# An attention kernel's score products as 32-row tiles, with zero products in TensorE's gaps, VectorE's exponentials in threes as E + E·v, and another start

## The chip, the cores and the metric

One Trainium2 chip; the program runs on one of its cores. The metric is the device time of one execution, in microseconds (us). The kernel before was run three times: 943.21, 945.67 and 946.64, median 945.67.

## The reference

Two attention blocks over the same input x (2048 rows of 512) are mixed by a gate: a softmax attention A with 32 heads of 16 and a linear attention B. Cut to what matters:

```python
q, k, v = ...                                   # x @ wqkv, 32 heads of 16
p = softmax(einsum("bhqd,bhkd->bhqk", q, k) * 16**-0.5)   # 32 x 2048 x 2048
a = einsum("bhqk,bhkd->bhqd", p, v) @ wo        # block A
...
phi = lambda t: where(t > 0, t + 1, exp(t)) + 1e-6        # block B, linear
o = (phi(q) @ (phi(k).T @ v)) / (phi(q) @ sum(phi(k)) + 1e-6)
g = sigmoid((x * gate_w).sum(-1))
return g * a + (1 - g) * (o @ wo_b)
```

Nearly all the work is in A: 32 x 2048 x 2048 = 134 million exponentials, and for each head a product with only 16 rows of contraction on the way in and only 17 columns (16 of v and a one, whose sum is the softmax's denominator) on the way out.

## The kernel before, in words

**Units.** The work of A is cut into 2048 units. A unit is one head, one block of 128 keys and one chunk of 512 queries: a score product with 128x512 results in one PSUM bank, the exponential of these 65,536 numbers, and four products with v (one for each 128 queries) that add into one PSUM bank, `acc`. 32 rounds of 64 units (4 heads, 16 key blocks) follow one another: 4 groups of eight heads (`t8`), 4 query chunks (`qc`), 2 halves (`half`). At a round's end VectorE divides by the sums (`round_end`, L942 to L971), and only then may the next round write `acc`.

**Score products.** K of eight heads lies on 128 partitions, 16 for each head (`KT`). Q of the four heads of a round is copied by DMA into `Qpad`, where the rows of other heads are zero, so that a product over 64 partitions (`ROWT = 64`, L20) picks one head out (`head_of` L146, `unit_aps` L893). Units that follow each other lie in different halves of TensorE's rows, and two such products can run side by side.

**Two ways to an exponential.** ScalarE takes units three at a time, a *group*: three score products into three banks (`SLOTS`, two sets of three), one `activation(Exp)` over 128x1536 into `PT` (L1337), then the v products from `PT`. VectorE takes the others, called *claims*: one score product into bank 7 (the one bank that is left, `MISC`), an eviction to fixed point (`YI`, L1084), and for each *pair* of claims four instructions over 128x1024 (`close_pair`, L1090): from the upper half of each number a power of two `E` (L1100), from the lower half a cubic polynomial in two steps `pol` (L1102, L1104), and the last step with the product by `E`, which gives `DP` (L1106). Then v products from `DP`.

**Who sets the order.** All instructions are written out by a planner in Python that keeps a clock for every engine (`PE.t`, `AC.t`, `DV.t`), estimated durations (L156 to L167: `LAT`, `QK3_T`, `PV_T`, `d_psum`, `d_sb`) and the time at which each buffer is written and read. On the chip each engine runs its own list in order; semaphores hold it where data is missing. The main loop (from L1306) takes one group a turn: the score products of group g, its activation, and then, as long as TensorE's planned clock is before the time `t_lim` at which the other three banks come free (L1346), it puts in other TensorE work. v products come first (`pv_step`, L984, 12 products for three units), then `misc_step` (L1208): a piece of a projection or of block B (`step_K`, `step_Q`, `step_V`, `step_BK` and so on, held in chains with a due group each) or a claim. Both need bank 7. A claim is made only while VectorE's planned backlog is under `CLAIM_LOAD` = 4.0, and from a round that has `MIN_LEFT` = 24 units left, from its end backwards. `pump` (L401) chooses VectorE's next instruction.

```python
            t_lim = max(max(r_bank[nb0 + k].tr for k in range(nbn)) + LAT, PE.t + 0.02)
            while PE.t < t_lim - 0.05:
                pump(PE.t)
                if pv_step(PE.t):
                    continue
                if PE.t + 0.2 < t_lim and g > last_stage and misc_step(PE.t):
                    continue
                PE.t += 0.05
```

**Start.** Half of x comes by plain DMAs on ScalarE's queue (`xnat`, which lies in `phiQT`) and is transposed on TensorE, half by eight transposing DMAs on SP's queue; then come the weights (L500 to L515). While the first 14 groups run, the projections of the other three quarters of x are put between them (`stage_fns`, L1269), and the gate's 64 products with one column each after group 13. TensorE's first work is 8 products of a zero tile (`warm`, L1253).

**End.** After the last activation come 28 products of the output projection for the last four blocks of 128 rows, the last transposes, four evictions and four stores (L1366 to L1404).

All TensorE products are issued at L490 (L493 for transposes), so the profile tells them apart by the names of their tiles.

Of the kernel before, what the change touches and what calls it, by code (L numbers as in the profile page):

```python
# [19 lines left out]
ROWT = 64  # L20
PVN = 64


A3, A2, A1, A0 = 0.07802452, 0.22606714, 0.69583353, 0.99992521
# [5 lines left out]
POLY_B = A2 / A3 * 2.0 ** 16  # L30
POLY_C = A1 / A3 * 2.0 ** 32
POLY_D = A0 / A3 * 2.0 ** 48
# [113 lines left out]
def head_of(half, j):  # L146

    if ROWT == 128:
        h = 4 * half + j
        return h, 0, j  # L150
    if ROWT == 64:
        return 2 * j + half, 64 * (j // 2), j % 2
    return 2 * j + half, 32 * j, 0


LAT = 0.13  # L156
MM512 = 0.216
QK3_T = {32: 0.25, 64: 0.43, 128: 0.65}[ROWT]
PV_T = 0.115
# [6 lines left out]
def d_sb(n, rate=1.0):  # L166
    return 0.10 + n * 1.042e-3 * rate  # L167


def bass_gated_mix__mha_block__linear_attn_block__prompt_kernel(  # L170
# [20 lines left out]
    NPT = 5  # L191
    NDP = 4
    NQS = 4
    NOUTT = 4

    with ExitStack() as es:
# [19 lines left out]
        pidx_i = SB([128, 1], I32, "pidxi")  # L216
        hidx_f = SB([128, 1], FP32, "hidxf")
        mtmp = SB([128, 8], FP32, "mtmp")
        maskK = SB([128, 8], FP32, "maskK")
        maskQ = SB([128, 4], FP32, "maskQ")  # L220
# [3 lines left out]
        NQI = ROWT // 32  # L224
        Qpad = SB([128, NQS, NQI, 512], BF16, "Qpad")
        VW = 32 if PVN == 64 else 18
        Vraw = SB([128, 2 * NTB * 8 * VW + 32], BF16, "Vaug")
        Vaug = Vraw[:, 0:2 * NTB * 8 * VW].rearrange("p (a t h c) -> p a t h c", a=2, t=NTB, h=8)
        PT = SB([128, NPT, 1536], BF16, "PT")
        YI = SB([128, 2, 1024], I32, "YI")  # L230
        E16 = SB([128, 2, 1024], I16, "E16")
        pol = SB([128, 2, 1024], FP32, "pol")
        DP = SB([128, NDP, 1024], BF16, "DP")
# [5 lines left out]
        upool = SB([128, 2, 512], BF16, "upool")  # L239
        phiK = SB([128, 2, 4, D], BF16, "phiK")  # L240
# [4 lines left out]
        phiQT = SB([128, 2, NCC, 512], BF16, "phiQT")  # L245
# [22 lines left out]
        semXN = [SEM("s_xn0"), SEM("s_xn1")]  # L268
        semW0 = SEM("s_w0")
# [16 lines left out]
        r_xnat = [R(f"xnat{i}") for i in range(2)]  # L286
        r_wA, r_wA0, r_warm, r_wB, r_woA, r_woB = R("wA"), R("wA0"), R("warm"), R("wB"), R("woA"), R("woB")
        r_gw, r_ident, r_const, r_mask, r_bmask, r_dummy = R("gw"), R("ident"), R("const"), R("mask"), R("bmask"), R("dm")
        r_KT = [[R(f"KT{p}_{t}") for t in range(NQC)] for p in range(2)]
        r_Qs = [R("Qs0"), R("Qs1")]  # L290
        r_Q = [R(f"Q{s}") for s in range(NQS)]
        r_V = [[R(f"V{p}_{v}") for v in range(NQC)] for p in range(2)]
        r_PT = [R(f"PT{i}") for i in range(NPT)]
        r_YI = [R("YI0"), R("YI1")]
        r_E16 = [R("E0"), R("E1")]
        r_pol = [R("pol0"), R("pol1")]
# [6 lines left out]
        r_u = [R("u0"), R("u1")]  # L303
# [3 lines left out]
        r_phiQT = [[R(f"phiQT{p}_{i}") for i in range(NCC)] for p in range(2)]  # L307
# [161 lines left out]
        def pe_macro(fns, reads=(), writes=(), dur=0.2):  # L469
            settle(reads, writes)  # L470
            st = est_start(PE, reads, writes)
# [9 lines left out]
            for res in writes:  # L481
                res.w = ev
                res.r = {}
                res.tw = st + dur + 0.05
                res.we = PE
            PE.t = st + dur
            return ev

# [10 lines left out]
        for hh in range(2):  # L499
            dma(xnat[:, hh * (NTB // 2):(hh + 1) * (NTB // 2), :],  # L500
                x2[hh * (S // 2):(hh + 1) * (S // 2), 128 * (NCC - NCP):D].rearrange("(tb p) c -> p tb c", p=128),
                semXN[hh], writes=[r_xnat[hh]], total_after=16, E=AC, lands=6)
        for k3 in range(3):
            dma(wA0[:, :, k3, :], wsrc[:, :, k3 * D:k3 * D + 128], semW0, writes=[], total_after=48, E=AC)
        r_wA0.w = _Raw(semW0, 48)
        r_wA0.tw = 11.0
        dma(gw[:], gate_w.rearrange("(cc p) -> p cc", p=128), semG, writes=[r_gw], total_after=16, noncontig=True, E=AC,
            lands=12)
        NCD = NCC - NCP
        for t in range(NQC):  # L510
            for cc in range(NCD):
                dma(xT[:, cc, 512 * t:512 * (t + 1)], x2[512 * t:512 * (t + 1), 128 * cc:128 * (cc + 1)], semXT[cc][t],
                    writes=[r_xT[cc][t]], total_after=16, transpose=True, E=SP, lands=5 + 1.2 * (2 * t + cc))
        dma(wA[:], wsrc, semW1, writes=[r_wA], total_after=16, lands=20)
        dma(wB[:], B_wqkv.rearrange("(cc p) n -> p cc n", p=128), semW2, writes=[r_wB], total_after=16, lands=24)  # L515
        dma(woA[:], A_wo.rearrange("(i p) n -> p i n", p=128), semW3, writes=[r_woA], total_after=16, lands=26)
        dma(woB[:], B_wo.rearrange("(i p) n -> p i n", p=128), semW4, writes=[r_woB], total_after=16, lands=28)
        xt_all = [r_xT[c][t] for c in range(NCC) for t in range(NQC)]

        def xt_of(t):  # L520
            return [r_xT[c][t] for c in range(NCC)]

# [6 lines left out]
        op(PO, lambda: nc.gpsimd.iota(pidx_i[:], [[0, 1]], base=0, channel_multiplier=1), writes=[r_const])  # L529
# [102 lines left out]
        def w_of(t8, kind, early):  # L632
            if early:
                return (lambda cc: wA0[:, cc, kind, :]), r_wA0
# [835 lines left out]
```

## Time and profile before

| what | value |
|---|---|
| profiled execution, its own time | 949.2 us |
| its span, first to last instruction | 947.4 us |
| ScalarE busy | 862.7 us, 91% |
| TensorE busy (products) | 858.0 us, 91% |
| VectorE busy | 742.3 us, 78% |
| mean granted TensorE clock | 0.969 |
| first activation of a group starts / last one ends | 16.88 / 935.43 us |
| groups on ScalarE; units claimed by VectorE | 611; 215 |
| ScalarE waits for TensorE, in all | 64.6 us, 107 times |
| VectorE waits for a claim's product, in all | 127.1 us, 118 times |

The table of groups gives for each line of the kernel, engine and pair of tiles the number of instructions, their busy time, the mean of one in ns and the idle time of the engine ahead of them. The page's row of digits shows the span in 40 slices, with a row for the clock that TensorE was granted. The view of stages gives the same for any stretch, with the busy time and, after "x", the instructions of each engine; its last three columns are the granted clock, the share of the DMA engines and GB/s. The view in order of time gives the start, the length, the engine and line, the tiles and the count of like instructions that follow one another. Busy times of products overlap each other: what one costs TensorE is read from one start to the next.

### The profile page before, as it was taken

To read this page: it belongs to the slowest core of one execution; us is meant where nothing else is said; L and a number is where in the kernel's file an instruction comes from. 1 tells how busy PE (TensorE), PEld (TensorE's weight loads), DVE (VectorE), ACT (ScalarE), POOL (GpSimd) and SP (SyncE) were. 2 spreads that over 40 slices of the span, in tenths; PEclk is the share of its full clock that TensorE was granted. 3 is DMA by queue.
4 is the path that set the end of the run, shared out by engine and by line. 5 is a ranking of instruction groups with operands and counts; after the bars stand their busy time and mean duration, and the time that the engine had idled before them with its cause. 6 is when DMAs were issued, how large, how long until landed. Compare 5 with 4: busy or idle time off the path is not lost. (4 is left out here: it accounts for less than half of the span.)

```text
span 947.4 us, 25379 instructions
## 1 busy us (share of the span) xinstructions
PE 858.0 (91%) x11144; PEld 422.3 (45%) x11244; DVE 742.3 (78%) x982; ACT 862.7 (91%) x648; POOL 8.8 (1%) x46
## 2 busy tenths in 40 slices
PE   7998988998999898999999988999998999988997
PEld 2544444444444444454444444444444444344443
DVE  4269787778888878878878988877888988687872
ACT  2789899999999989999999999979999999999995
POOL 3000000000000000000000000000000000000000
PEclk7989899999999999999999999979999999999999
DMA  9000000000000000000000001000010011000001
GB/s 277 10 8 7 7 1 10 5 7 6 3 12 2 9 6 7 7 2 7 4 10 7 2 14 23 13 2 7 7 24 14 18 19 29 18 19 12 12 13 35
DMA packets 33902, 16.52 MB, mean 17 GB/s; under 512 B 25664, under 2 KB 32768, under 8 KB 33792
## 3 DMA queue, kind: packets, MB, share of 16 engines
q1 hardware_dynamic: 29600, 13.45, 5.7%
q8 instruction: 89, 1.46, 0.7%
q10 hardware_dynamic: 4192, 1.44, 0.6%
q14 instruction: 21, 0.17, 0.1%
HBM read 5.64 MB, written 2.10 MB: 8 GB/s over the span
## 5 line engine op out<-in xcount | busy, mean ns | idle before, releaser
L1337 ACT ACTIVATE PT<-ps 128x1536 bf16<-128x1536 f32 x611 | 846.6, 1458 | 67.1 <-PE ps L490 64.6
L490 PE MATMUL ps<-Qpad,KT 64*128 64x512 bf16 x2048 | 418.4, 390 | 14.2 <-DVE YI L1084 8.3
L490 PEld LDWEIGHTS ps<-Vaug,PT 128*128 128x128 bf16 x7332 | 255.7, 99 | 251.9 <-PE ps L490 232.7
L490 PE MATMUL ps<-Vaug,PT 128*128 128x64 bf16 x7332 | 330.3, 196 | 5.1 <-DVE Osb L968 0.5
L1084 DVE TENSOR_SCALAR YI<-ps 128x512 int32<-128x512 f32 x215 | 147.8, 687 | 127.9 <-PE ps L490 127.1
L490 PEld LDWEIGHTS ps<-Qpad,KT 64*128 64x128 bf16 x2048 | 83.9, 94 | 142.3 <-issue 64.2
L1104 DVE SCALAR_TENSOR_TENSOR pol<-pol,YI 128x1024 f32<-128x1024 f32 x108 | 131.4, 1216 | 2.8
L1106 DVE SCALAR_TENSOR_TENSOR DP<-pol,E 128x1024 bf16<-128x1024 f32 x108 | 131.0, 1213 | 1.0
L1102 DVE SCALAR_TENSOR_TENSOR pol<-YI 128x1024 f32<-128x1024 uint16 x108 | 130.9, 1212 | 0.0
L1100 DVE TENSOR_SCALAR E<-YI 128x1024 int16<-128x1024 int16 x108 | 74.6, 690 | 3.4
L490 PE MATMUL ps<-Vaug,DP 128*128 128x64 bf16 x860 | 45.2, 195 | 27.1 <-DVE DP L1106 13.2
L490 PEld LDWEIGHTS ps<-Vaug,DP 128*128 128x128 bf16 x860 | 32.6, 98 | 64.0 <-DVE DP L1106 32.2
L490 PE MATMUL ps<-wB,xT 128*128 128x512 bf16 x96 | 31.2, 379 | 10.0 <-DVE YI L1084 6.4
L490 PE MATMUL ps<-xT,wA 128*128 128x512 bf16 x83 | 27.3, 385 | 8.4 <-DVE YI L1084 4.6
L742 DVE COPY tpool<-ps 128x512 f32<-128x512 f32 x32 | 21.9, 683 | 2.9 <-PE ps L490 2.9
L490 PE MATMUL ps<-wA,xT 128*128 128x128 bf16 x192 | 19.5, 226 | 1.8 <-DVE YI L1084 0.6
L875 DVE CAST outt<-ps 128x512 bf16<-128x512 f32 x12 | 8.3, 691 | 16.2 <-PE ps L490 16.2
L701 DVE CAST Vaug<-ps 128x512 bf16<-128x512 f32 x16 | 11.0, 687 | 12.1 <-PE ps L490 12.1
L739 ACT ACTIVATE epool<-tpool 128x512 bf16<-128x512 f32 x32 | 20.2, 631 | 0.2 <-DVE tpool L742 0.2
L490 PE MATMUL ps<-xT,wB 128*128 128x512 bf16 x49 | 15.8, 379 | 3.8 <-DVE YI L1084 2.5
L490 PE MATMUL ps<-woB,OBT 128*128 128x512 bf16 x51 | 15.6, 379 | 4.1 <-DVE YI L1084 3.0
L644 DVE CAST KT<-ps 128x512 bf16<-128x512 f32 x16 | 11.0, 684 | 8.3 <-PE ps L490 8.3
(72 smaller groups left out, 243.5 us busy)
## 6 DMA issues: line engine op xcount, KB each, us to landing
out_dram<-outt SPq DMA_DIRECT2D x16, 128.0 KB, 1.7
Qpad<-Qs SPq DMA_DIRECT2D x124, 16.0 KB, 1.8
wA<-in_A_wqkv_dram SPq DMA_DIRECT2D x1, 1536.0 KB, 7.1
wB<-in_B_wqkv_dram SPq DMA_DIRECT2D x1, 1536.0 KB, 10.4
phiQT<-in_A_x_dram ACTq DMA_DIRECT2D x2, 512.0 KB, 4.9
woA<-in_A_wo_dram SPq DMA_DIRECT2D x1, 512.0 KB, 11.4
woB<-in_B_wo_dram SPq DMA_DIRECT2D x1, 512.0 KB, 12.5
outt<-in_A_wqkv_dram ACTq DMA_DIRECT2D x3, 128.0 KB, 5.5
```

Source lines behind the costliest of these rows:

```text
L490: return lambda: nc.tensor.matmul(o, lhsT=l, rhs=r, start=start, stop=stop, skip_group_check=sg)
L644: push(1, [(lambda: nc.vector.tensor_copy(KT[:, par, 512 * t:512 * (t + 1)], bank_ap(b)), [r_bank[b]], [r_KT[par][t]], d_psum(512), None)])
L701: push(1, [(lambda: nc.vector.tensor_copy(Vaug[:, par, 4 * v:4 * v + 4, :, 0:16], src), [r_bank[b]], [r_V[par][v]], d_psum(512), lambda: v ...
L739: _emit(AC, lambda: nc.scalar.activation(epool[:, s, :], tpool[:, s, :], ACT.Exp), [r_t[s]], [r_e[s]], 0.6, 0.53)
L742: (lambda: nc.vector.tensor_copy(tpool[:, s, :], bank_ap(b)), [r_bank[b]], [r_t[s], r_e[s]], d_psum(512), after),
L875: push(1, [(lambda: nc.vector.tensor_copy(outt[:, s, :], bank_ap(b)), [r_bank[b]], [r_outt[s], r_wA0], d_psum(512), lambda: store_out(tb))])
L1084: push(1, [(lambda: nc.vector.tensor_scalar(YI[:, yi, 512 * k:512 * (k + 1)], bank_ap(b), Y_LO * FRAC, Y_HI * FRAC, op0=ALU.max, op1=ALU.min),
L1100: (lambda: nc.vector.tensor_scalar(e16, hi, float(EXP_OFF + 127), 128.0, op0=ALU.add, op1=ALU.mult), [r_YI[yi]], [r_E16[yi]], d_sb(n, 0.5) ...
L1102: (lambda: nc.vector.scalar_tensor_tensor(out=pl, in0=lo, scalar=POLY_B, in1=lo, op0=ALU.add, op1=ALU.mult), [r_YI[yi]], [r_pol[yi]], d_sb ...
L1104: (lambda: nc.vector.scalar_tensor_tensor(out=pl, in0=pl, scalar=POLY_C, in1=lo, op0=ALU.add, op1=ALU.mult), [r_YI[yi], r_pol[yi]], [r_pol ...
L1106: (lambda: nc.vector.scalar_tensor_tensor(out=DP[:, dp, 0:n], in0=pl, scalar=POLY_D, in1=e16.bitcast(BF16), op0=ALU.add, op1=ALU.mult), [r ...
L1337: op(AC, lambda slot=slot, b0=b0, n=n: nc.scalar.activation(PT[:, slot, 0:n], ps[:, 512 * b0:512 * b0 + n], ACT.Exp, scale=LN2 / FRAC, bia ...
```

## The change

- **Score products** run over 32 partitions (`Qpad` is 512 columns for a round, one mask) in place of 64. The units of a group are three of the four heads j, so they lie in three of the four row tiles.
- **Claims** are of key blocks 12 to 15 only. A claim may be issued right behind a group's three products, of a head in the fourth row tile (`claim_beside`); one by itself is made only at a lower backlog (`LATE_CLAIM` 2.5). A round must have 38 units left (30 the last), where it was 24.
- **VectorE's arithmetic**: three claims make a *triple*, with instructions over 128x1536. The polynomial is normalised so that the exponential is E·D + E·v with a constant D: `pol` (one `scalar_tensor_tensor`), E, v = (pol + C)·lo (another one), and w = v·E as a `tensor_tensor` on bf16. The sum is made by TensorE: a claim's v products are run twice, with E against `V2` (v times D, a second copy that is written for key blocks 12 to 15) and with w against `Vaug`.
- **Zero products**: where the planner has time before `t_lim` and the planned products of the last 3 us fill less than `MAC_LOW` = 0.45 of it, it adds a product of the zero tile into `acc` (`fill`), 512 columns over 128 rows. It can't while `acc` is between rounds.
- **Order**: new estimates of durations; a latest time `t_late` for other work ahead of a group's products; `misc_step` goes ahead of `pv_step` unless more than 12 units wait for their v products; six `PT` buffers for five, three `DP` of three units for four of two.
- **Start**: the first 512 rows of x come whole in one DMA on ScalarE's queue (into two `PT` buffers) and are transposed on TensorE, with copies by VectorE and ScalarE in turn; first weights in three DMAs ahead of all else on SP's queue; the other rows as before, in smaller pieces; the first K is evicted by ScalarE; GpSimd makes the masks with selects and does most of the memsets; 9, 4 and 2 zero products stand around the first projections.
- `phiQT` now lies in `phiK`; `upool` is gone (in place in `epool`).

```diff
-ROWT = 64
-A3, A2, A1, A0 = 0.07802452, 0.22606714, 0.69583353, 0.99992521
+PB, PC, PD = 2.8964260871, 8.9161113650, 12.8125
+NTRI = 3
+KB2 = 12
-LAT = 0.13
-QK3_T = {32: 0.25, 64: 0.43, 128: 0.65}[ROWT]
-PV_T = 0.115
+LAT = 0.11
+QK_T = 0.324
+PV_T = 0.12
+SWITCH_T = 0.095
...
+        def pe_macro(fns, reads=(), writes=(), dur=0.2, mac=0.0, rows=128):
             settle(reads, writes)
+            if rows < pe_rows[0]:
+                PE.t += SWITCH_T
+            pe_rows[0] = rows
...
         def unit_aps(r, u):
             t8, qc, half = rounds[r]
-            kb, j = unit(r, u)
-            h, row, i = head_of(half, j)
-            kt = KT[row:row + ROWT, t8 % 2, 128 * kb:128 * (kb + 1)]
-            q = Qpad[row:row + ROWT, r % NQS, i, :]
+            kb, j = u // 4, u % 4
+            kt = KT[32 * j:32 * j + 32, t8 % 2, 128 * kb:128 * (kb + 1)]
+            q = Qpad[32 * j:32 * j + 32, r % NQS, :]
...
             push(3, [
-                (lambda: nc.vector.tensor_scalar(e16, hi, float(EXP_OFF + 127), 128.0, op0=ALU.add, op1=ALU.mult),
-                 [r_YI[yi]], [r_E16[yi]], d_sb(n, 0.5), None),
                 (lambda: nc.vector.scalar_tensor_tensor(out=pl, in0=lo, scalar=POLY_B, in1=lo, op0=ALU.add, op1=ALU.mult),
-                 [r_YI[yi]], [r_pol[yi]], d_sb(n), None),
-                (lambda: nc.vector.scalar_tensor_tensor(out=pl, in0=pl, scalar=POLY_C, in1=lo, op0=ALU.add, op1=ALU.mult),
-                 [r_YI[yi], r_pol[yi]], [r_pol[yi]], d_sb(n), None),
-                (lambda: nc.vector.scalar_tensor_tensor(out=DP[:, dp, 0:n], in0=pl, scalar=POLY_D, in1=e16.bitcast(BF16),
-                                                        op0=ALU.add, op1=ALU.mult),
-                 [r_pol[yi], r_E16[yi]], [r_DP[dp]], d_sb(n), None)])
+                 [r_YI[yi]], [r_pol], d_sb(n), None),
+                (lambda: nc.vector.tensor_scalar(e16, hi, float(EXP_OFF + 127), 128.0, op0=ALU.add, op1=ALU.mult),
+                 [r_YI[yi]], [r_E16[dp]], d_sb(n, 0.5), None),
+                (lambda: nc.vector.scalar_tensor_tensor(out=w, in0=pl, scalar=POLY_C, in1=lo, op0=ALU.add, op1=ALU.mult),
+                 [r_YI[yi], r_pol], [r_DP[dp]], d_sb(n), None),
+                (lambda: nc.vector.tensor_tensor(w, w, eb, ALU.mult), [r_DP[dp], r_E16[dp]], [r_DP[dp]], d_sb(n, 0.5), None)])
             for k, (r, u) in enumerate(us):
-                pv_pending.append((r, u, DP[:, dp, 512 * k:512 * (k + 1)], r_DP[dp]))
+                sl = slice(512 * k, 512 * (k + 1))
+                pv_pending.append((r, u, [(eb[:, sl], True), (w[:, sl], False)], r_DP[dp]))
...
+        def fill(now):
+            if acc_n[0] == 0 or r_acc.pend:
+                return False
+            pe_macro([f_mm(acc, warm[:, 0:128], warm[:, 0:512], start=False, stop=False, sg=True)], reads=[r_warm],
+                     writes=[r_acc], dur=MM512, mac=0.216)
+            return True
...
             t_lim = max(max(r_bank[nb0 + k].tr for k in range(nbn)) + LAT, PE.t + 0.02)
+            t_late = max(t_lim, AC.t - (QK_T + SWITCH_T + 0.06 + LAT + MARGIN))
             while PE.t < t_lim - 0.05:
                 pump(PE.t)
-                if pv_step(PE.t):
+                behind = sum(1 for e in pv_pending if len(e[2]) == 1) > PV_LAG
+                if behind and PE.t + 0.3 < t_late and pv_step(PE.t):
                     continue
-                if PE.t + 0.2 < t_lim and g > last_stage and misc_step(PE.t):
+                if g > last_stage and misc_step(PE.t, t_late):
+                    continue
+                if not behind and PE.t + 0.3 < t_late and pv_step(PE.t):
+                    continue
+                if PE.t + 0.25 < t_lim and mac_share(PE.t) < MAC_LOW and fill(PE.t):
                     continue
                 PE.t += 0.05
```

## The prediction

> **What bounds the kernel now.** I read the page's busy shares first, then the groups, then the order of time in a good and in a bad stretch, then stages. Whole-page shares put ScalarE and TensorE level:
>
> ```profile
> span 947.4 us, 25379 instructions
> PE 858.0 (91%) x11144; PEld 422.3 (45%) x11244; DVE 742.3 (78%) x982; ACT 862.7 (91%) x648; POOL 8.8 (1%) x46
> ...
> PEclk7989899999999999999999999979999999999999
> ...
> L1337 ACT ACTIVATE PT<-ps 128x1536 bf16<-128x1536 f32 x611 | 846.6, 1458 | 67.1 <-PE ps L490 64.6
> L490 PE MATMUL ps<-Qpad,KT 64*128 64x512 bf16 x2048 | 418.4, 390 | 14.2 <-DVE YI L1084 8.3
> ...
> L1084 DVE TENSOR_SCALAR YI<-ps 128x512 int32<-128x512 f32 x215 | 147.8, 687 | 127.9 <-PE ps L490 127.1
> ```
>
> ScalarE's activations are the long chain, and what they wait for is TensorE; so do VectorE's claims. How fast ScalarE could go is seen where nothing holds it:
>
> ```profile
> 924.58 10.85 ACT L1337 ACTIVATE PT<-ps 128x1536 bf16<-128x1536 f32 x8
> ...
> 928.93 0.60 PE L490 MATMUL ps<-Qpad,KT 64*128 64x512 bf16 x3
> 929.46 0.41 PEld L490 LDWEIGHTS ps<-Vaug,PT 128*128 128x128 bf16 x12 [0.42 <-PE ps L490]
> 929.46 0.52 PE L490 MATMUL ps<-Vaug,PT 128*128 128x64 bf16 x12
> 929.80 0.13 PEld L490 LDWEIGHTS ps<-woA,OT 128*128 128x128 bf16 x2
> ```
>
> Eight activations in 10.85 us, the last one 1.46 long: (10.85 - 1.46)/7 = 1.34 from start to start, since they overlap by 0.12. The median start-to-start over the trace is 1.33; I use 1.335. The whole span then divides so: 16.9 us to the first activation; 611 x 1.335 = 815.7; 32 activations of block B at 0.63 less the overlap, 16.3; 12.0 after the last one (935.4 to 947.4); the rest, 86, is lost between activations. By the stage they fall in (distance between starts, less 1.335): 14.5 up to 60 us, 18.5 in and around the stretches where the clock is halved, 53 over the other 564 groups, 0.094 a group. The page's 64.6 us of waits is less than this, as each break also loses the overlap.
>
> TensorE from one start to the next, at full clock: three score products 929.46 - 928.93 = 0.53, their v products 0.34 to 0.36, so 0.89 of 1.335 for a group; a claim's product 0.2 and its v products 0.12, 0.35 of them a group (215/611), 0.11; projections and block B about 96 us over 611 groups, 0.16. That makes 1.16, spare 0.17: any piece of 0.53 (two products of 512 columns) in the wrong place makes the next group late. That is the bound: ScalarE, held up by a nearly full TensorE.
>
> The bad stretch, in windows of 3.41 us (the granted clock is the third number from the end; it changes only at multiples of this length):
>
> ```profile
> 619.60:623.01 3.41, 3.09 (x49) 1.66 (x50) 1.66 (x3) 3.41 (x3) 0.00 (x0) 1.00 0.01 2
> 623.01:626.43 3.42, 3.02 (x44) 1.40 (x41) 3.35 (x5) 3.42 (x4) 0.00 (x0) 1.00 0.02 5
> 626.43:629.84 3.41, 2.36 (x28) 1.01 (x27) 3.07 (x6) 3.41 (x3) 0.00 (x0) 1.00 0.00 0
> 629.84:633.26 3.42, 3.30 (x35) 1.82 (x35) 0.00 (x0) 1.38 (x2) 0.00 (x0) 0.50 0.00 0
> ```
>
> At a round's end TensorE idles 1 us for `acc`, and the clock halves for 10.2 us. I counted in each such window the products' columns times their share of the 128 rows (512 columns over 128 rows fill 0.219 us: two take 0.528, one 0.309). The six windows of the main loop ahead of a fall are filled to 0.23 to 0.35; of the windows between, none under 0.376; their median is 0.61. So in this trace the clock falls when less than about 0.36 of the array's time is filled, although TensorE is 70% busy in that window.
>
> **The change, part by part.**
>
> 1. Score products. A pair in different halves costs one stream: four products take 0.54, three 0.53, so 0.219 each stream and 0.1 fixed. Three row tiles side by side should be 0.53 - 0.219 = 0.32. Bounds: 0.32, and 0.53 if they don't overlap further. A claim behind them rides in the fourth tile, 0 to 0.2. v products stay 0.36; a claim's are doubled, 0.24. With 0.43 claims a group: 0.32 + 0.36 + 0.10 + 0.16 = 0.94 of 1.335. Spare 0.39 for 0.17.
>
> 2. Waits of ScalarE. With twice the spare room and a latest time for other work, 0.094 a group should shrink, between 0 and 0.094. The nearest row is today's best stage, 240 to 300 us: 42 groups and 4 activations of block B in 60 us lose 1.9 us, 0.045 a group. I take 0.05: 53 becomes 29. What is late next there is `acc` at the round's end, unchanged.
>
> 3. VectorE. A pair costs 2 x 0.687 + 0.690 + 1.212 + 1.216 + 1.213 = 5.705, 2.85 a unit. Triples, from the rows at 1024 and 512 columns (0.693 and 0.417; 1.217 and 0.69): E 0.96, the two three-operand steps 1.745 each, evictions 2.06. The bf16 product isn't in the trace: 0.96 if it runs like E (two-byte, SBUF), 1.745 if like the three-operand steps; I take 0.96, as its operands are two-byte like E's. Sum 7.47, 2.49 a unit (2.75 the other way). VectorE's other work is 742.3 - 615.7 = 126.6. In 110 to 340 us it is busy 190 of 230, and 37 of the idle 40 is the wait for a claim's product; with claims that cost TensorE no turn I take 0.87 of some 870 us: 757 - 120 = 637, 256 units. At today's 0.826: 240; at 0.93 some 276; at the dear product and 0.826, 217. So (2048 - 256)/3 = 597 groups (591 to 610): 14 x 1.335 = 18.7 less. The second V copy, 4 x 0.69 on VectorE, is in the 120.
>
> 4. Clock. Filled per group after: 3 x 0.055 for scores, 0.33 for v, 0.43 x (0.055 + 0.22) for claims, over 1.40, plus projections 0.11: 0.54 on average for 0.60 before, nearer to 0.36. The zero products cost TensorE 0.22 each in time that is spare by the plan, and lift poor windows; they can't run while `acc` changes hands, which is where it fell. Cost of a cold us today: 2.3 lost for 3.4, 5.7 for 10.2, so 0.6. The loss of 18.5 may go to 0 or stay; I take 10.
>
> The rule against this: TensorE: Matmul & The Clock Gate (The HAM clock gate; HAM oscillation) has the clock fall after an idle window of about 3.4 us. By it neither kernel would fall in the main loop, and the loss would be 0, 10 us better than my sum. The windows above contradict it: the longest gap there is 1 us. And TensorEngine Tiling (Key Properties) says that a change of tiling mode drains TensorE. The fixed 0.1 above agrees; this kernel pays it already, in each group, and full-height zero products beside the 32-row ones would only add turns in spare time.
>
> 5. Start. Today: transposes at 5.05, then 3.7 us until VectorE is through its memsets and the copies, first projection at 9.40, eight cold products of 0.5, first activation 16.88. After: x whole at 5.0 to 5.6 (today's x loads land in 4.9 of issue at 0.73), four sets of transposes and copies to 7.0, Q 0.9 (1.7 cold), K 0.9 (1.7), eviction 0.7, score products to activation 0.65 (1.07), 0.2 between. 10.4 warm, 12.4 cold; I take 11.0, 5.9 less. SP's transposing DMAs now stand behind three weight loads, some 3 us later, and are needed two groups later than the first activation; ScalarE's two copies and one eviction lie ahead of its first group.
>
> 6. First 60 us: 14.5 lost, part of it cold. The same stretch's warm groups lose 0.5 for a K step, 1.2 for a V step, 1.4 for the gate: three of each and the gate, 6.5; I take 7 (5 to 14.5). End: unchanged, 12.0 (up to 17 if VectorE's last triple, 5.4 us, comes late).
>
> **Sum**, for the profiled execution: 11.0 + 597 x 1.335 (797.0) + 16.3 + 7 + 10 + 29 + 12.0 = 882.3 of span. Before, the execution took 949.2 for 947.4 of span, and the median of the runs lies 3.5 under it: 882.3 + 1.8 - 3.5 = 881.
>
> **Rivals.**
>
> - *The waits stay* (0.22): the plan's clocks and the chip's differ as before, or `acc` and bank 7 hold things up rather than TensorE's fill. Then 0.094 a group, 18.5 for the clock and 10 for the start stay, claims gain only VectorE's cheaper arithmetic at the dear end (606 groups) and the first activation is at 12: 12 + 809 + 16.3 + 10 + 18.5 + 53 + 12 - 1.7 = 929. For it: best stretches are already without loss. Against: 36.8 us of 37 are VectorE waiting for TensorE.
> - *The clock stays down* (0.08), the one that ends slower: 32-row products fill so little that the zero products, barred between rounds, don't hold 0.36. At 0.6 a cold us, the 66 gained are gone after 110 us more of it (12% of the span); with a quarter of the span cold, 881 + 0.6 x 200 = 1001. For it: 0.54 for 0.60, and falls at round ends. Against: windows without projections have the most spare time, and one zero product a group lifts a window by 0.16.
> - *The gain is no gain* (0.05): the row tiles don't overlap further (0.53 stays), doubled v products take what claims gave back, and VectorE gets no more units: within 10 us of today.
>
> Chances: forecast 0.65. Faster by over 0.5% (about what a measurement of this kernel can tell from none): 0.65 + 0.22 = 0.87; within 0.5% 0.04; slower 0.08 + 0.01. Range: low end from 10.4 + 591 x 1.335 + 16.3 + 5 + 0 + 17 (0.03 a group) + 12 - 1.7 = 848; high end the first rival, 930.
>
> **What would show it.** Three score products to the next start 0.32, not 0.53. Starts of activations 1.335 apart for most, breaks well under 141. About 256 claims, 85 triples, the bf16 product at 0.96. First activation near 11. A clock at 1.0 from the start on; falls, if any, at round ends. I am wrong if the page's clock row shows many digits under 9, if ScalarE waits for TensorE over 50 us in all, or if VectorE stays near 0.8 busy.

## The result, and the profile after

The changed kernel takes 886.05 us in the median of four runs (884.01 to 888.74). The kernel before, on the same chip, takes 946.15 (943.21 to 954.32). The ratio is 0.9354, with an interval of 0.929 to 0.9417. The forecast was 881, with a range of 848 to 930. Medians and ranges count every run; the ratios leave out those more than 1.5% above the kernel's quickest.

The profiled execution took 884.01 us for a span of 882.3. The page, with the lines that answer to those shown of before:

```profile
span 882.3 us, 27338 instructions
PE 783.2 (89%) x12209; PEld 447.8 (51%) x12311; DVE 729.9 (83%) x909; ACT 839.1 (95%) x642; POOL 9.1 (1%) x19
...
PEclk8889999999999999999989999999999999999999
...
L1402 ACT ACTIVATE PT<-ps 128x1536 bf16<-128x1536 f32 x602 | 823.9, 1490 | 23.1 <-PE ps L504 19.9
L504 PE MATMUL ps<-Qpad,KT 32*128 32x512 bf16 x2048 | 275.8, 389 | 34.5 <-ACT PT L1402 15.5
L1098 DVE TENSOR_SCALAR YI<-ps 128x512 int32<-128x512 f32 x244 | 167.5, 687 | 81.5 <-PE ps L504 80.9
...
L1116 DVE SCALAR_TENSOR_TENSOR pol<-YI 128x1536 f32<-128x1536 uint16 x82 | 143.0, 1744 | 2.6
L1120 DVE SCALAR_TENSOR_TENSOR DP<-pol,YI 128x1536 bf16<-128x1536 f32 x82 | 142.4, 1736 | 0.0
...
L1118 DVE TENSOR_SCALAR E<-YI 128x1536 int16<-128x1536 int16 x82 | 77.3, 943 | 0.0
L1122 DVE TENSOR_TENSOR DP<-DP,E 128x1536 bf16<-128x1536 bf16 x82 | 77.2, 941 | 0.2
```

ScalarE is at 95%, and its wait for TensorE has gone from 64.6 to 19.9 us: it is the bound almost alone now (802 of the 882 us are its whole groups at their own pace, see the table below). VectorE takes 244 units for 215, and its wait for a claim's product went from 127.1 to 80.9 us. Its four steps of a triple cost 943, 941, 1744 and 1736 ns in the mean. The clock row has its digits under 9 at the start and one in the middle.

A good stretch in order of time, 202 to 219 us:

```profile
202.21 0.10 PEld L504 LDWEIGHTS ps<-warm 128*128 128x128 bf16 x1 [0.35 <-PE ps L504]
...
202.53 0.10 PEld L504 LDWEIGHTS ps<-Qpad,KT 32*128 32x128 bf16 x4 [0.23 <-issue]
202.54 0.40 PE L504 MATMUL ps<-Qpad,KT 32*128 32x512 bf16 x4
...
202.87 0.52 PE L504 MATMUL ps<-Vaug,PT 128*128 128x64 bf16 x12
...
207.74 14.98 ACT L1402 ACTIVATE PT<-ps 128x1536 bf16<-128x1536 f32 x11
```

Four score products, three of a group and one of a claim behind them, start at 202.54 and the next product at 202.87: 0.33 us, where three took 0.53. Not all fours are as short: half of them take 0.41 us or more. A zero product stands ahead of them in TensorE's free time. The eleven activations in 14.98 us are (14.98 - 1.46)/10 = 1.35 apart: ScalarE runs through.

Dividing both profiled spans in the same way, each loss being the distance between activations' starts less 1.335:

| term of the span, us | before | forecast | after |
|---|---|---|---|
| to the first activation | 16.9 | 11.0 | 13.2 |
| whole groups x 1.335 | 611: 815.7 | 597: 797.0 | 601: 802.3 |
| block B's activations, one short group | 16.3 | 16.3 | 18.5 |
| lost before 60 us | 14.5 | 7 | 11.7 |
| lost at a halved clock, after 60 us | 18.5 | 10 | 4.0 |
| other losses after 60 us | 53 | 29 | 18.4 |
| after the last whole activation | 12.0 | 12.0 | 14.1 |
| sum | 947 | 882.3 | 882.2 |

Of the 65 us between the spans, 35 are waits, 14.5 the clock, 13.4 ten groups fewer, and the start gives 6.6; block B and the end cost 4.3 more. The sum agrees with the forecast far better than its terms do; the misses are taken up below.

Where a number below is called the fill of a window, it is counted as in the prediction, by weight loads (their records are complete; some products' are missing): columns times rows, 0.219 us for 512 columns over 128 rows, in windows of 3.41 us aligned with the clock's changes.

### The profile page after: what moved, and what is told of

Read it like the earlier page. It is cut to its first block, busy times and chain, and to the rows that moved or that the text cites. A ratio compares the mean times of both kernels' runs of the same rounds, so it can differ in the third digit from the quotient of the medians.

```text
span 882.3 us, 27338 instructions
## 1 busy us (share of the span) xinstructions
PE 783.2 (89%) x12209; PEld 447.8 (51%) x12311; DVE 729.9 (83%) x909; ACT 839.1 (95%) x642; POOL 9.1 (1%) x19
## 4 chain that ended last, share of the span: by engine, by line
PE 53%; DVE 22%; issue 12%; ACT 12%; DMA 1%; ACTq 0%
PE ps L504 52%; ACT PT L1402 11%; DVE YI L1098 5%; DVE DP L1120 4%; DVE pol L1116 3%; DVE E L1118 2%; DVE DP L1122 1%; DVE tpool L766 1%; DVE Osb L986 1%; ACT epool L763 1%; DVE OB L869 1%; DMA PT<-in_A_x_dram 1%; DVE rden L984 0%; DVE phi L769 0%; DVE Vaug L720 0%
## 5 line engine op out<-in xcount | busy, mean ns | idle before, releaser
L1402 ACT ACTIVATE PT<-ps 128x1536 bf16<-128x1536 f32 x602 | 823.9, 1490 | 23.1 <-PE ps L504 19.9
L504 PE MATMUL ps<-Qpad,KT 32*128 32x512 bf16 x2048 | 275.8, 389 | 34.5 <-ACT PT L1402 15.5
L1098 DVE TENSOR_SCALAR YI<-ps 128x512 int32<-128x512 f32 x244 | 167.5, 687 | 81.5 <-PE ps L504 80.9
L1116 DVE SCALAR_TENSOR_TENSOR pol<-YI 128x1536 f32<-128x1536 uint16 x82 | 143.0, 1744 | 2.6
L1120 DVE SCALAR_TENSOR_TENSOR DP<-pol,YI 128x1536 bf16<-128x1536 f32 x82 | 142.4, 1736 | 0.0
L504 PEld LDWEIGHTS ps<-Qpad,KT 32*128 32x128 bf16 x2048 | 67.5, 91 | 126.3 <-issue 39.1
L504 PE MATMUL ps<-Vaug,E 128*128 128x64 bf16 x976 | 66.4, 195 | 19.2 <-DVE Osb L986 10.3
L1118 DVE TENSOR_SCALAR E<-YI 128x1536 int16<-128x1536 int16 x82 | 77.3, 943 | 0.0
L1122 DVE TENSOR_TENSOR DP<-DP,E 128x1536 bf16<-128x1536 bf16 x82 | 77.2, 941 | 0.2
L504 PEld LDWEIGHTS ps<-Vaug,E 128*128 128x128 bf16 x976 | 44.7, 98 | 50.1 <-PE ps L504 31.6
L769 DVE SCALAR_TENSOR_TENSOR phi<-tpool,epool 128x512 bf16<-128x512 f32 x32 | 21.9, 683 | 0.3
```

The costliest lines, as they stand in the source:

```text
L504: return lambda: nc.tensor.matmul(o, lhsT=l, rhs=r, start=start, stop=stop, skip_group_check=sg)
L769: (lambda: nc.vector.scalar_tensor_tensor(out=dst, in0=tpool[:, s, :], scalar=0.0, in1=epool[:, s, :], op0=ALU.max, op1=ALU.add), [r_t[s], ...
L1098: push(1, [(lambda: nc.vector.tensor_scalar(YI[:, yi, 512 * k:512 * (k + 1)], bank_ap(b), Y_LO * FRAC, Y_HI * FRAC, op0=ALU.max, op1=ALU.min),
L1116: (lambda: nc.vector.scalar_tensor_tensor(out=pl, in0=lo, scalar=POLY_B, in1=lo, op0=ALU.add, op1=ALU.mult), [r_YI[yi]], [r_pol], d_sb(n), ...
L1118: (lambda: nc.vector.tensor_scalar(e16, hi, float(EXP_OFF + 127), 128.0, op0=ALU.add, op1=ALU.mult), [r_YI[yi]], [r_E16[dp]], d_sb(n, 0.5) ...
L1120: (lambda: nc.vector.scalar_tensor_tensor(out=w, in0=pl, scalar=POLY_C, in1=lo, op0=ALU.add, op1=ALU.mult), [r_YI[yi], r_pol], [r_DP[dp]], ...
```

## The experiments

All ratios are to the kernel before, run on the same chip. Theory: the 32-row products give TensorE the room, the fill decides the clock, and the zero products keep what the room gains. Rivals: the clock follows TensorE's idleness and the zero products do nothing; or the gain is the new order's alone.

### No zero products in the main loop

```diff
-        MAC_LOW = 0.45
+        MAC_LOW = 0.0
```

> The kernel after, without the 76 zero products of the main loop; those of the start stay. Theory (the clock falls when a window of 3.41 us is filled to less than about 0.36 by columns times rows): counted on the trace after, the zero products are what keeps 6 windows above 0.36 and 14 above 0.40, so there should be 6 to 14 falls in the main loop in place of 2, each some 6 us long at 0.4 us lost per cold us: 15 to 30 us slower than after, 900 to 915. Rival (zero data, or full-height products in spare time, do nothing for the clock, and the plan's latest time does it all): within 3 us of after, 883 to 889.

897.26 us, ratio 0.951 (0.9447 to 0.9573). Groups (602), the start (11.5 lost) and the small losses (17.1) stay; the clock falls 8 times after 60 us for 2, and 17.0 us are lost there for 4.0. Its clock row:

```profile
PEclk8898989989999999999999899999999989999999
```

The 13 us more at a halved clock are the whole difference of the spans (894.0 less 882.3). By the medians, this kernel is 11 us slower, less than the theory's 15 to 30. Without zero products the planner also comes to another order after the first tenth of TensorE's list, so this run alone does not part the zero products from the order; the run with zero products over 32 rows, below, keeps the order.

### 64-row score products in the changed kernel

```diff
-QK_T = 0.324
+QK_T = 0.535
...
-            kb, j = u // 4, u % 4
-            kt = KT[32 * j:32 * j + 32, t8 % 2, 128 * kb:128 * (kb + 1)]
-            q = Qpad[32 * j:32 * j + 32, r % NQS, :]
+            kb, j = u // 4, (0, 2, 1, 3)[u % 4]
+            kt = KT[64 * (j // 2):64 * (j // 2) + 64, t8 % 2, 128 * kb:128 * (kb + 1)]
+            q = Qpad[64 * (j // 2):64 * (j // 2) + 64, r % NQS, :]
```

(A product over these 64 rows adds the scores of two heads; the work and the sizes are those of 64-row tiles.)

> The kernel after with score products over 64 rows, as before, and the planner told so (0.535 for three, 0.108 of fill each). It takes the 64 rows from the same tile as the 32, so a score is the sum of two heads' scores and the output is not the reference's; instructions, sizes and waits are the same. Theory (TensorE's turn is what held ScalarE): TensorE's time for a group goes up by 0.21 to about 1.15 of 1.335, claims drop below those of before (198 by the order, 617 groups), waits come back: 940 to 985. Rival (the new order with its latest time for other work made the gain, the height of the tiles did little): under 905.

1005.6 us, ratio 1.064 (1.0552 to 1.0727): slower than before, and than both expected. From its page:

```profile
span 1003.8 us, 26868 instructions
PE 899.1 (90%) x12059; PEld 450.0 (45%) x12059; DVE 626.5 (62%) x799; ACT 863.2 (86%) x657; POOL 9.1 (1%) x19
...
L1402 ACT ACTIVATE PT<-ps 128x1536 bf16<-128x1536 f32 x617 | 846.1, 1476 | 97.1 <-PE ps L504 92.7
L504 PE MATMUL ps<-Qpad,KT 64*128 64x512 bf16 x2048 | 397.5, 395 | 49.4 <-DMA Qpad<-Qs 30.0
```

VectorE falls to 62% and 198 units, ScalarE waits 92.7 us for TensorE, a wait for Q's copies appears, as Q's projections came late, and 37 us follow the last activation, as output projections were left over. Divided as above, 75 us are lost beside a halved clock (18.5 before): it falls 11 times after 60 us, six of them beside those waits for Q, the longest of which leave TensorE idle for 4.4 to 4.6 us. The other losses after 60 us are 31 us, 0.057 a group, less than the 0.094 of before. So the new order by itself is no gain. Its projections come late; that the doubled v products and the claims beside groups use up their room is the likely reason, which no run took apart.

### 32-row score products alone, in the kernel before

The planner's duration is kept at 0.43, so that TensorE's, ScalarE's and SP's lists are those of before.

```diff
-ROWT = 64
+ROWT = 32
-QK3_T = {32: 0.25, 64: 0.43, 128: 0.65}[ROWT]
+QK3_T = {32: 0.43, 64: 0.43, 128: 0.65}[ROWT]
```

> The kernel before with score products over 32 rows and the planner's estimates untouched, so TensorE's, ScalarE's and SP's lists are the same instruction for instruction. Theory: waits shrink (53 to about 25), but with half the rows 26 to 47 of the 253 windows of before would be filled to less than 0.36 to 0.40, so the clock falls some 25 times or more, 150 to 250 us of it cold at 0.4 to 0.6 us each: no faster than before, 940 to 1000, mean clock below 0.93. Rival (the tiles alone make the gain, and rows don't count for the clock): 900 to 920 at a clock of 0.97.

952.03 us in the median of ten runs, ratio 1.004 (0.9988 to 1.0091): no difference. This is where a large change moves the time little, and its page shows where the gain went:

```profile
span 950.9 us, 25479 instructions
...
PEclk6778797898999999989979986797888989998799
...
L1337 ACT ACTIVATE PT<-ps 128x1536 bf16<-128x1536 f32 x611 | 840.2, 1483 | 78.2 <-PE ps L490 76.4
```

The clock fell 23 times after 60 us, for 5 before, and was halved for 215 us of the span. The losses that lie apart from a halved clock went from 53 to 11.7, over the 435 groups that are left there; those beside a halved clock went from 18.5 to 64.3. So the room is real, and all of it is paid back, while the mean fill of the full-clock windows fell from 0.62 to 0.51.

### (pol + D)·E as one step, one set of v products

```diff
-                (lambda: nc.vector.scalar_tensor_tensor(out=w, in0=pl, scalar=POLY_C, in1=lo, op0=ALU.add, op1=ALU.mult),
-                 [r_YI[yi], r_pol], [r_DP[dp]], d_sb(n), None),
-                (lambda: nc.vector.tensor_tensor(w, w, eb, ALU.mult), [r_DP[dp], r_E16[dp]], [r_DP[dp]], d_sb(n, 0.5), None)])
+                (lambda: nc.vector.scalar_tensor_tensor(out=pl, in0=pl, scalar=POLY_C, in1=lo, op0=ALU.add, op1=ALU.mult),
+                 [r_YI[yi], r_pol], [r_pol], d_sb(n), None),
+                (lambda: nc.vector.scalar_tensor_tensor(out=w, in0=pl, scalar=POLY_D, in1=eb, op0=ALU.add, op1=ALU.mult),
+                 [r_pol, r_E16[dp]], [r_DP[dp]], d_sb(n), None)])
...
-                pv_pending.append((r, u, [(eb[:, sl], True), (w[:, sl], False)], r_DP[dp]))
+                pv_pending.append((r, u, [(w[:, sl], False)], r_DP[dp]))
```

> The kernel after with VectorE's arithmetic of before, in threes: (pol + D) * E as one three-operand step, one set of v products for a claim. Theory (VectorE's time per claim sets how many it takes): 2.75 us a unit for 2.49, 216 claims for 244, 611 groups for 602: 9 x 1.335 = 12 us more, 895 to 900. Rival (the doubled v products cost TensorE what VectorE gains, 244 x 0.12 = 29 us of its time): as fast as after or faster, 875 to 888.

897.78 us, ratio 0.9477 (0.9395 to 0.956); 611 groups and 216 claims. The theory's time came, but not by its cause alone. The profiled execution, the longest of the four (906.04), has this clock row:

```profile
PEclk8879989989999899999997968999979999999999
```

The clock falls 10 times after 60 us. Against the changed kernel's profile the nine groups more are 12 us, the loss at a halved clock is 28 us for 4.0, and the other losses after 60 us are 4 us for 18.4. So at full clock the kernel with one set of v products is held up some 14 us less, about what its nine groups cost: there the rival has its price. What the second set gives besides is fill (without zero products 0.53 here, 0.56 in the changed kernel). No profile shows the other three executions; their granted clock was 0.955 to 0.965, for 0.975 to 0.982 in the changed kernel. Hence the next run.

### The same, with more zero products

`MAC_LOW` = 0.60 in the kernel above: 250 zero products in the main loop for 125.

> The kernel with (pol + D) E as one three-operand step and one set of v products, and in addition zero products up to a planned fill of 0.60 (250 in the main loop instead of 125). It has 611 groups and 216 claims for 602 and 244. Theory (its 12 us are nine groups more): with a full clock it still takes 895 to 898. Rival (its 12 us were the colder clock, as it has fewer v products to fill TensorE): with the clock held it comes to 884 to 889, so that the split sum is worth nothing on VectorE.

909.15 us, ratio 0.9589 (0.9546 to 0.9632): neither. The profile (the quickest of the six, a span of 898.8) against that of the changed kernel on another chip (876.9, below): 9 groups more are 12.0 us, and 16.9 us are lost at a halved clock, in 7 falls after 60 us, for 4.0. The other losses after 60 us are up from 4 to 17 us, with 250 zero products for 125. So the clock was not held, and the 250 products did not replace what the second set of v products filled. Whether the split sum gains anything by VectorE's time alone stays open: no run has one set of v products and a full clock.

### Zero products over 32 rows

The same 76 products, in the same places, of the same 512 columns:

```diff
-            pe_macro([f_mm(acc, warm[:, 0:128], warm[:, 0:512], start=False, stop=False, sg=True)], reads=[r_warm],
+            pe_macro([f_mm(acc, warm[0:32, 0:128], warm[0:32, 0:512], start=False, stop=False, sg=True)], reads=[r_warm],
```

> The changed kernel, the 76 zero products of its main loop taken over 32 rows instead of 128: the same order of everything, the same number of products, the same columns, a quarter of the rows. Theory (what holds the clock is columns times rows): each adds 0.055 us of fill instead of 0.219, so the clock falls nearly as often as without them: 6 to 9 falls in the main loop, 12 to 17 us lost to the cold clock, 894 to 899 us. Rival (what holds the clock is that TensorE streams something, rows or not): two falls or three as in the changed kernel, 885 to 888 us.

898.47 us, ratio 0.952 (0.9478 to 0.9562), as without any (0.951). The clock row and ScalarE's line, from the longest of its six executions (907.11; the others 895 to 903):

```profile
PEclk8879969999988989999999879979999999999999
...
L1402 ACT ACTIVATE PT<-ps 128x1536 bf16<-128x1536 f32 x602 | 825.3, 1498 | 43.9 <-PE ps L504 41.1
```

Nine falls after 60 us, and 29 us lost at a halved clock. TensorE's list is that of the changed kernel, product for product, with as many columns, and the clock does not hold. So rows count: the rival, that streaming is what matters, is out. As the order is the same here, this run is also the cleaner measure of what full-height zero products are worth: 12 us by the medians.

### More zero products, and fewer

`MAC_LOW` = 0.60 (168 in the main loop), and 0.35 (15):

> The changed kernel with a zero product wherever the planned fill of the last windows is under 0.60 instead of 0.45: 168 instead of 76, 603 groups. Theory: the clock does not fall in the main loop, or once (0 to 1.5 us lost instead of 4.0), but each product of 0.22 us makes something late now and then and one more group costs 1.3, so the gain is given back: 884 to 888. Rival: zero products cost their time, 92 x 0.22 = 20 us more at most, 890 to 906.

896.3 us, ratio 0.9486 (0.9457 to 0.9516): the rival. Two falls, as with 76, and the small losses go from 18.4 to 30.3 us, the breaks between activations from 76 to 106. That is 0.13 us for each of the added 92 products; most likely few of them found a free gap, but the planner's order is another one too.

> The changed kernel with zero products only where the planned fill of the last windows is under 0.35 instead of 0.45: 15 in the main loop instead of 76, 603 groups. Without any it took 897, with 168 it took 896. Theory (the fill decides, and most falls come from windows between 0.30 and 0.40): 5 to 7 falls, 890 to 896. Rival (a few, in the emptiest windows, are enough): 2 or 3 falls, 884 to 888.

908.01 us, ratio 0.9601 (0.9554 to 0.9649): worse than either theory, and no better than without any (0.951, up to 0.9573).

```profile
PEclk8889989799999899789999999999979699999999
```

Twelve falls after 60 us, 33.7 us lost there. With another limit the planner arranges all that follows differently, and this order is emptier by itself: without its zero products 22 of its full-clock windows are filled under 0.40, against 17 in the changed kernel's order and 13 in the one without zero products. Why its order comes out so is open. That the 15 products, for a planned fill under 0.35, cover too few of the windows that fall is the likely reading: eleven of the twelve falls came after windows filled to 0.33 or more.

### The start and the end

```diff
-    NOUTT = 3
+    NOUTT = 4
...
-        run_now(step_V(0, 0, early=True))
-        stage = {}
+        stage = {0: [lambda: run_now(step_V(0, 0, early=True))]}
```

> The changed kernel with two edits at its ends: the first V projection (16 products) goes behind the first group instead of ahead of it, and there are four output buffers instead of three. Theory: group 0 waited at 12.72 us for the eviction of that V, and K's eviction was over at 10.48, so the first activation starts near 11.1 instead of 13.16; the second-last output eviction no longer waits 1.73 us for an output transfer, so 12 to 12.5 us follow the last activation instead of 14.1. Both gained: 882 to 883 for 886. Rival: V's 1.8 us stand in front of group 1 or 2 all the same and are lost inside the first 60 us (13.5 instead of 11.65 lost there), so that only the end is gained: 884.5.

883.38 us, ratio 0.9349 (0.9315 to 0.9383): not to be told from the changed kernel. ScalarE in order of time, first the changed kernel, then this one:

```profile
9.90 0.58 ACT L661 CAST KT<-ps 128x512 bf16<-128x512 f32 x1 [2.49 <-PE ps L504]
13.16 4.13 ACT L1402 ACTIVATE PT<-ps 128x1536 bf16<-128x1536 f32 x3 [2.67 <-PE ps L504]
```

```profile
10.99 1.45 ACT L1401 ACTIVATE PT<-ps 128x1536 bf16<-128x1536 f32 x1 [0.49 <-PE ps L504]
14.27 2.79 ACT L1401 ACTIVATE PT<-ps 128x1536 bf16<-128x1536 f32 x2 [1.83 <-PE ps L504]
```

The first activation starts at 10.99, as the prediction had it, and the second waits 1.83 us behind the V that was moved: 15.0 us are lost before 60 us for 11.7. The rival was right for the start, where the loss is even 1.5 us more than it said. At the end 12.7 us follow the last activation of all (870.31) for 13.6 (868.68 in the changed kernel): 0.9 of the 1.7 expected.

### Zero products in the first groups, and a control

The control is the changed kernel itself. The second kernel has four output buffers and this; the third has V behind group 0 besides:

```diff
+            if g <= 6 and acc_n[0] == 0:
+                pe_macro([f_mm(acc, warm[:, 0:128], warm[:, 0:512]) for _ in range(2)], reads=[r_warm],
+                         writes=[r_acc], dur=2 * MM512, mac=2 * 0.216)
             for k, (r, u) in enumerate(us):
                 pv_pending.append((r, u, [(PT[:, slot, 512 * k:512 * (k + 1)], False)], r_PT[slot]))
```

> The changed kernel as it is, on the same chip as the three others of this call, to compare with. Expected within 883 to 889 us and a ratio to before of 0.935 within 0.004.

> The changed kernel with four output buffers, and with two zero products into acc behind the score products of each of the first groups, until the first attention-value product opens acc; the first V projection stays ahead of group 0. Theory (the 11.65 us lost before 60 us are in part the halved clock of 14.6 to 28.2, which began after a window filled to 0.305): no fall there, 7 to 9 us lost before 60 us, 12 to 12.5 us after the last activation, 880 to 883. Rival (that stretch is held by the order of K, V and transposes in it, and zero products only stand in the way): 11 to 14 us lost, 884 to 888.

> The same, and the first V projection behind group 0. Theory: with the clock full, V and the score products of group 1 take half as long and part of the 2.1 us of the earlier first activation is kept: first activation near 11.0, 9 to 10 us lost before 60 us, 879 to 882. Rival: V's products and the eviction of its bank are in the way of group 1 at any clock, and the earlier start is given back as with the full-length loss of 15: within 1 us of the kernel with V ahead, or above it.

| kernel, same chip | median (range of six runs) | ratio | clock, by run |
|---|---|---|---|
| the change | 888.03 (878.58 to 890.83) | 0.9386 (0.9339 to 0.9433) | 0.971 to 0.992 |
| early zero products, four buffers | 879.07 (878.59 to 883.73) | 0.9301 (0.926 to 0.9342) | 0.984 to 0.992 |
| and V behind group 0 | 883.51 (879.64 to 888.59) | 0.9337 (0.929 to 0.9384) | 0.977 to 0.992 |

The control's profiled execution was its quickest, and it shows one reason why the change's runs differ. Its page, then that of the second kernel:

```profile
span 876.9 us, 27440 instructions
...
PEclk9999999999999999999989999999999999999999
...
L1402 ACT ACTIVATE PT<-ps 128x1536 bf16<-128x1536 f32 x602 | 822.7, 1488 | 18.6 <-PE ps L504 15.6
```

```profile
span 877.1 us, 27464 instructions
...
PEclk9999999999999999999999999999999999999999
...
L1402 ACT ACTIVATE PT<-ps 128x1536 bf16<-128x1536 f32 x602 | 822.8, 1489 | 19.2 <-PE ps L504 16.3
```

The same program as in the first profile, and the clock did not fall at 14.6 us: 7.2 us are lost before 60 us where it was 11.7. What differs is where the windows lie against the program. In the seven profiles of the changed order whose windows begin 0.7 to 2.0 us after the span's start or a multiple of 3.41 later, one window near 11 us is filled to 0.27 to 0.40 and the clock falls; in the three at 2.4 to 2.9 it does not. In both profiles with early zero products (0.1 and 3.2) it does not fall either, so the profiles alone do not separate the cure from luck: the second kernel loses 7.8 us before 60 us, the control 7.2. But all six runs of the second kernel lie at 878.6 to 883.7, and five of the control's six lie at 884 to 891. That is 1% faster than the change on the same chip, with intervals that just touch, and some 0.9 us of it are the fourth buffer's; of what was run it is the quickest kernel. V behind group 0 loses 13.8 us before 60 us in the profile taken and gains nothing: the rival again.

## Why the prediction was right, and which terms were not

**Score products**: right. Three to the next start take 0.324 in the median (0.32 forecast), and that is the room from which the waits went: the 32-row products in the kernel before show it, where the losses at full clock fell from 0.094 to 0.027 a group. The claim behind them was summed at 0, within 0 to 0.2, and that was too cheap: of the 232 fours at full clock 105 take 0.33, but 108 over 0.5, for waits or for the claim's own turn; the mean is 0.51, so 0.18 for the claim.

**Waits of ScalarE**: right in kind, too dear. 0.033 a group in place of 0.05: 18.4 us for 29. The value was near that of the best stretch of before (0.045); the changed kernel does better than that stretch.

**VectorE's arithmetic**: right, a unit costs 2.48 us (7.43 a triple; 2.49 forecast), and the bf16 product takes 0.947, the cheap end (0.96). What the cheaper unit is worth as a whole is less clear: the run with one set of v products takes nine groups more, 12 us, and has 14 us less of small losses. **Its share**: wrong. 244 units for 256, VectorE at 83% for 87%, so four groups more, 5.3 us. The step that failed was to say that a claim which costs TensorE no turn leaves VectorE without waits: it still waits 80.9 us for products. Where evictions of claims follow each other within 3 us, they begin 1.52 us apart in the median (1.65 before), though one takes 0.69, and groups come each 1.33. That they wait for bank 7 and the next group's turn is the likely reason; no run took it apart.

**Clock**: the mechanism was right, and the loss 4.0 for 10. The prediction let 0 to 18.5 stand, and only the zero products made the low end: without them it is 17.0. The second rival, the clock staying down, was given 0.08; it is what the 32-row products do on their own, though not with its price: in the old kernel with 32-row products 188 us at the halved clock after 60 us cost 64, 0.34 each and not 0.6, probably as TensorE had more room there. The rule that lets the clock fall after an idle window of 3.4 us, weighed in the prediction, fails again. In the changed kernel's own bad stretch, in windows (the granted clock third from the end):

```profile
448.06:451.47 3.41, 2.14 (x46) 1.35 (x43) 3.34 (x8) 3.41 (x5) 0.00 (x0) 1.00 0.09 19
451.47:454.88 3.41, 3.26 (x39) 1.76 (x38) 1.28 (x3) 2.70 (x3) 0.00 (x0) 0.50 0.16 39
454.88:458.30 3.42, 3.30 (x48) 2.31 (x45) 1.27 (x2) 2.02 (x2) 0.00 (x0) 0.50 0.09 24
```

In the window ahead of the fall TensorE is busy for 2.14 of 3.41 us, its longest gap is 1.2 us, and it is filled to 0.40.

**Start**: wrong by 2.2 us, and 4.7 more before 60 us. "Score products to activation 0.65" left out that V's 16 products and the eviction of its bank stood ahead of group 0:

```profile
10.13 1.76 PE L504 MATMUL ps<-outt,xT 128*128 128x128 bf16 x16
12.72 0.39 PE L504 MATMUL ps<-Qpad,KT 32*128 32x512 bf16 x3 [0.83 <-DVE Vaug L720]
```

K was there at 10.48; group 0 waited for VectorE to empty the bank that V had filled. The two runs that move V behind group 0 did not win the 2.2 us all the same: there V's 1.8 us stand in front of group 1. "A clock at 1.0 from the start on" was wrong in this execution and nearly right in the control's, where it falls once before 60 us, at 36.6 for 3.4 us, and the loss is 7.2 for the 7 forecast.

**End**: 14.1 for 12.0. "Unchanged" passed over the output buffers, of which the changed kernel has three for four; the last eviction waits for a store. First the kernel before, then the changed one:

```profile
943.26 1.07 ACT L1404 CAST outt<-ps 128x512 bf16<-128x512 f32 x2 [7.83 <-PE ps L490]
```

```profile
877.25 0.58 ACT L1477 CAST outt<-ps 128x512 bf16<-128x512 f32 x1 [8.57 <-PE ps L504]
879.56 0.59 ACT L1477 CAST outt<-ps 128x512 bf16<-128x512 f32 x1 [1.73 <-DMA out_dram<-outt]
```

With four, the two evictions run without a break, for 0.9 us less. The short last group is another 0.5, and 0.7 is the longer wait for TensorE's last products, 8.57 us for 7.83, whose cause is open.

So the terms that were too dear (the waits by 10.6, the clock by 6) made up for those that were too cheap (the start by 6.9, groups and block B by 7.5, the end by 2.1). The forecast was right in its mechanism and in most of its prices. That the spans agree to 0.1 us is luck: 16.6 us of error one way and 16.5 the other. The 5 us between 881 and 886 come from the step from span to median, for which 3.5 was taken off; here the profiled execution was the quickest of the four.

## What to carry to other kernels

Before smaller row tiles are used to make room on TensorE, count the fill, columns times rows in windows of 3.4 us: the room is worth nothing while a halved clock takes it back. Full-height zero products keep the clock, and pay only as long as they stand in true gaps: here 76 were worth 11 to 12 us, and an order with 92 more lost 10. And take the parts of such a change together as well as alone: here the row tiles alone gave nothing, the new order without them lost 6%, and both with the zero products gained 6.5%. An order written out by a planner can change as a whole with one limit, so the best test of a part keeps the order, as the zero products over 32 rows did.

## What the runs showed of the hardware

The fill at which the clock falls, over the 14 profiles, in the windows at full clock from 60 us to 20 us before the end:

| fill of the window | windows | clock halved after it |
|---|---|---|
| under 0.30 | 18 | 18 |
| 0.30 to 0.35 | 31 | 26 |
| 0.35 to 0.40 | 95 | 45 |
| 0.40 to 0.45 | 200 | 8 |
| 0.45 to 0.50 | 277 | 2 |
| 0.50 and over | 2552 | 0 |

The prediction's edge of 0.36 was the low side of a band; it is not sharp, and what else decides inside it these runs do not show. Products over 32 and 128 rows in turn cost no more than the 0.1 us a group that was there with 64 rows (0.324 less a stream of 0.219).

The section on the clock gate in the Trainium skill, TensorE: Matmul & The Clock Gate (The HAM clock gate), says that the activity window runs freely and does not begin with the kernel. The control agrees: the same program met it in another place and lost 7.2 us in place of 11.7 before 60 us. That an idle window is what halves it does not agree: of the 99 falls counted above, 81 came after windows filled to 0.30 or more.
